# k^T v on column halves of TensorE, k's maximum by GpSimd for chunks 3 to 8, and q's transposes and k^T v issued as one piece

## The chip, the cores and the metric

The kernel runs on one core of one Trainium2 chip. The metric is device microseconds (us) of the whole launch; three runs of the kernel before gave 907.95, 908.01 and 909.28, median 908.01. No other core works beside it.

## The reference

A linear attention feeds a feed-forward layer (FFN). The inputs q, k and v have 8 batches, 8 heads, 576 rows and 64 columns; the FFN has 4608 tokens, 512 columns in and out, 2048 hidden units. All is float32.

```python
q_s = exp(q - max(q, -1)); q_s = q_s / (sum(q_s, -1) + 1e-09)
k_s = exp(k - max(k, 2)); k_s = k_s / (sum(k_s, 2) + 1e-09)
kv = einsum('bhsd,bhse->bhde', k_s, v)
x = einsum('bhsd,bhde->bhse', q_s, kv)      # then x to (4608, 512)
h = x @ w_in
g = where(h >= 1, h, where(h <= -1, 0, (h + 1) ** 2 / 4))
out = g @ w_out
```

q's maximum runs along the 64 columns of a row, k's along the 576 rows of a column.

## The kernel before

The 4608 tokens are cut into 9 chunks of 512, which the code counts from 0 (so its `c == 1` is the second chunk, and the title's chunks 3 to 8 are `c` = 2 to 7). In each chunk the FFN runs as 16 units, one for each 128 hidden units. A unit's first product (L608, tile h) is 12 matmuls of 128x512, its second (L646, tiles o) again 12; each float32 operand is split into a high and a low part in the type float32r, and three of the four products of parts are taken. Between the two products stand, on ScalarE and VectorE (ACT and DVE in the profile) in turn, `g_relu`, `g_square`, `g_min`, `g_hi` and `g_lo`; the second product needs gh, and in its third matmul gl. TensorE (PE) does the first product of the next unit before the second of this one.

The attention for chunk c+1 is worked in between, during chunk c, in four pairs of heads (`attention`, a pair is `pr`). For each pair and for `c` from 1 to 7 one batch of k and v is reduced to a 128x128 block kv, of which the two 64x64 blocks on the diagonal are wanted, one for each head:

- `k_max` (DVE) takes the maximum of the five row blocks of k, which leaves 128 partitions to be reduced. That is done on PE and DVE: `k_mt` (L382) transposes the 128x128 tile m1 into PSUM, `k_mc` (L386) takes the maximum of each row, `k_mb` (L390) transposes it back, broadcast over the partitions. `k_sub` (L394, DVE) and `k_exp` (L399, ACT) follow.
- `kv_mm` (L405) multiplies k^T by v in five float32 matmuls, each of which the profile shows as two passes, of 130 columns: 128 of v and two columns of ones, whose sum is the divisor. Of the 128x128 result half is thrown away.
- `kv_z`, `kv_hi` and `kv_lo` divide by the sum and split the blocks into parts.
- For q: `q_max` (DVE), `q_rows("qm")` (GpSimd, POOL in the profile), `q_exp` (ACT), `q_sum` (DVE), `q_rows("qrz")` (POOL), `q_tr` (L474, four transposes on PE), `q_hi`, `q_lo`, then `x_mm` (L498), `x_hi`, `x_lo`.

Chunk `c == 0` works otherwise (k comes transposed, its maximum is a free-axis one), and the ninth chunk has no k of its own. While chunk 0 runs, the weights come in as 32 pieces that ACT, DVE and POOL (`low`, L266) turn into high and low parts.

The order on each engine is fixed when the program is built. `Plan.order` is a list scheduler: each step has an engine, a booked time, a due time, and the steps it waits for; `do` gives a step its due time as a stage of its pair (`base`, in units of STEP = 5.5). Each engine then runs its own list strictly in order, so a step that waits holds up all that stand behind it. The booked times set the order alone.

Of the kernel before, what the change touches and what calls it, by code (L numbers as in the profile page):

```python
# [3 lines left out]

# [146 lines left out]
def tile_linear_attention_then_ffn(  # L151
# [18 lines left out]
    nc = tc.nc  # L170
# [122 lines left out]
    def attention(c, pr, due, step, slack):  # L293
# [52 lines left out]
        def k_max():  # L346
            kt = t["k"]
            m2 = wk.tile([P, 2, P], F32, tag="m2", name=f"m2_{n}")
            nc.vector.tensor_tensor(m2, kt[:, 0:2, :], kt[:, 2:4, :], ALU.max)
            t["m1"] = m1 = m2[:, 0, :]  # L350
# [61 lines left out]

        def kv_z():
            if first:
                z = zs = t["zs"]
            else:
                z = sm.tile([P, 1], F32, tag="z", name=f"z_{n}")
                zs = t["kv"][:, P : P + 1]
            nc.vector.tensor_scalar(z, zs, EPS, None, ALU.add)
            t["rz"] = sm.tile([P, 1], F32, tag="rz", name=f"rz_{n}")  # L420
            nc.vector.reciprocal(t["rz"], z)

        def kv_f():
            for i in range(2):
                r = slice(i * D, (i + 1) * D)
                nc.scalar.activation(
                    kvf[r, pr, r], t["kv"][r, r], AF.Copy, scale=t["rz"][r]
                )

        def kv_hi():  # L430
            for i in range(2):
                r = slice(i * D, (i + 1) * D)
                nc.scalar.activation(  # L433
                    kvt[r, c % 2, pr, 0, r], t["kv"][r, r], AF.Copy, scale=t["rz"][r]
                )

        def kv_lo():
            for i in range(2):
                r = slice(i * D, (i + 1) * D)
                nc.vector.scalar_tensor_tensor(  # L440
                    kvt[r, c % 2, pr, 1, r],
                    t["kv"][r, r],
                    t["rz"][r],
                    f32(kvt[r, c % 2, pr, 0, r]),
                    ALU.mult,
                    ALU.subtract,
                )
# [71 lines left out]
        if has_k:  # L519
            if first:  # L520
                rk, rh = room("ld kFalse", NLOAD), room("ps h", 2)
                km = do("DVE", 0.78, 0, kt_max, lk)
                ke = do("ACT", 0.95, 1, kt_exp, km)
                kz = do("DVE", 0.32, 4, kv_z, ke)
                tr = do("PE", 0.65, 2, kt_tr, ke, *rpk.wait(), *rh.wait())
                rpk.take(tr)
                rh.take(tr)
                kc = do("ACT", 0.62, 2.5, kt_copy, tr, *rk.wait())
                rk.take(kc)
                kd = do("DVE", 0.22, 2.5, kt_tail, kc)  # L530
                rh.free(kd)
                mm = do("PE", 1.15, 3.5, kv_mm, kc, kd, lv)
            else:
                rm = room("wk m2", 1)
                km = do("DVE", 1.08, 0, k_max, lk, *rm.wait(), port=True)
                rm.take(km)
                mt = do("PE", 0.25, 1, k_mt, km, *rpk.wait())
                rpk.take(mt)
                rm.free(mt)
                mc = do("DVE", 0.28, 1.5, k_mc, mt)  # L540
                mb = do("PE", 0.25, 2, k_mb, mc)
                ks = do("DVE", 0.81, 2.5, k_sub, mb)
                ke = do("ACT", 0.74, 3, k_exp, ks)
                mm = do("PE", 1.15, 3.5, kv_mm, ke, lv)
                kz = do("DVE", 0.32, 4, kv_z, mm)
            rk.free(mm)
            rv.free(mm)
            parts = [kvread.get((c - 2, pr))]
            late = START + 8 if first else 0.0
            kh = do("ACT", 0.62, 4.2, kv_hi, kz, mm, *parts, late=late)  # L550
            kl = do("DVE", 0.57, 4.4, kv_lo, kh, late=late)
            kvdone[c, pr] = kl
            if first:
                early_users.extend((mm, tr))
            kvready = [kl]
            if first:
                kf = do("ACT", 0.62, 4, kv_f, kz, mm)
                kvready = [kf]
                rpk.free(kf, kl)
            else:  # L560
                rpk.free(kl)
        qm = do("DVE", 0.68, 0.5, q_max, lq)
        qs = do("POOL", 1.05, 1, q_rows("qm", ALU.subtract), qm, port=True)
        qe = do("ACT", 0.63, 2, q_exp, qs)
        qz = do("DVE", 1.06, 2.2, q_sum, qe)
        qn = do("POOL", 1.05, 3, q_rows("qrz", ALU.mult), qz, port=True)
        tr = do("PE", 0.5, 3.6, q_tr, qn, *rpq.wait())
        rpq.take(tr)
        rq.free(tr)
# [228 lines left out]
```

## Time and profile before

| | |
|---|---|
| median of three runs | 908.01 us |
| the profiled execution, its own time | 908.67 us |
| its span, first to last instruction | 906.9 us |
| mean granted TensorE clock | 0.997 of full |
| PE busy | 888.5 us, 98% |
| DVE, ACT, POOL busy | 445.2, 431.2, 139.4 us |

A row of the timeline gives the start, the busy time, the engine, the line, what is written from what, the shapes and how many instructions were merged; in square brackets stands how long the engine was idle before, and what ended that. Busy times of matmuls overlap: what one costs on PE is the distance of the starts, not its own busy time.

### The profile page before, as it was taken

How to read it: one execution, taken by the hardware profiler on the slowest of the kernel's cores; microseconds unless marked ns; L12 is line 12 of the kernel's file. 1: busy time of each engine (PE TensorE's matmuls, PEld its weight loads, DVE VectorE, ACT ScalarE, POOL GpSimd, SP SyncE). 2: the span in 40 equal slices, each digit the busy share in tenths (PEclk: the TensorE clock that was granted, in tenths of full speed). 3: DMA queues.
4: the chain of work that ended last, by engine and by line, in shares of the span. 5: the costliest groups of instructions: out<-in, count | busy, mean ns of one | idle time of the engine just before them, and what ended most of it. 6: DMA issues, size and time to landing. Idle time of an engine off the chain costs nothing.

```text
span 906.9 us, 10847 instructions
## 1 busy us (share of the span) xinstructions
PE 888.5 (98%) x4184; PEld 734.5 (81%) x4184; DVE 445.2 (49%) x859; ACT 431.2 (48%) x736; POOL 139.4 (15%) x112
## 2 busy tenths in 40 slices
PE   6889999999999999999999999999999999999997
PEld 5568888888888888888888888888888888888885
DVE  6999975444544444444544454445444443333222
ACT  6868754443544444444444444445444444343333
POOL 5555631011101111111101110011111111000000
PEclk9999999999999999999999999999999999999999
DMA  8656512111211011011211121111100010000001
GB/s 316 199 185 218 188 52 76 42 41 41 88 41 42 29 70 34 37 42 57 73 41 42 41 88 41 41 41 68 33 28 13 27 44 12 1 12 36 1 0 47
DMA packets 24244, 57.36 MB, mean 63 GB/s; under 512 B 2688, under 2 KB 2688, under 8 KB 24192
## 3 DMA queue, kind: packets, MB, share of 16 engines
q1 hardware_dynamic: 24192, 56.67, 18.6%
q8 instruction: 33, 0.54, 0.3%
q14 instruction: 19, 0.16, 0.1%
HBM read 47.22 MB, written 9.44 MB: 62 GB/s over the span
## 4 chain that ended last, share of the span: by engine, by line
PE 89%; DVE 5%; issue 2%; ACT 1%; POOL 1%; DMA 1%; SPq 0%; DVEq 0%; POOLq 0%
PE o L646 40%; PE h L608 40%; PE kv L405 4%; PE x L498 3%; PE tp L474 2%; DVE st L252 1%; DVE st L255 1%; DVE gl L635 1%; POOL wl L266 1%; DVE r L627 1%; DMA v<-in_v 1%; PE mb L390 0%; DVE qz L467 0%; PE mt L382 0%; ACT kvt L433 0%
## 5 line engine op out<-in xcount | busy, mean ns | idle before, releaser
L627 DVE SCALAR_TENSOR_TENSOR r<-h,r 128x512 f32<-128x512 f32 x144 | 99.5, 691 | 276.2 <-ACT r L624 276.0
L608 PE MATMUL h<-xl,wh 128*128 128x512 f32 x576 | 229.7, 399 | 4.3 <-DVE r L627 3.0
L646 PE MATMUL o<-wl,gh 128*128 128x512 f32 x576 | 231.8, 402 | 0.6 <-DVE kvt L440 0.5
L646 PE MATMUL o<-wh,gl 128*128 128x512 f32 x576 | 225.8, 392 | 1.3 <-DVE gl L635 1.2
L608 PE MATMUL h<-xh,wl 128*128 128x512 f32 x576 | 225.8, 392 | 0.0
L608 PE MATMUL h<-xh,wh 128*128 128x512 f32 x576 | 225.0, 391 | 0.0
L646 PE MATMUL o<-wh,gh 128*128 128x512 f32 x576 | 224.5, 390 | 0.0
L621 ACT ACTIVATE r<-h,half 128x512 f32<-128x512 f32 x144 | 99.2, 689 | 244.3 <-PE h L608 243.5
L631 ACT CAST gh<-r 128x512 fp32r<-128x512 f32 x144 | 89.4, 621 | 88.9 <-DVE r L627 88.9
L646 PEld LDWEIGHTS o<-wh,gl 128*128 128x128 f32 x576 | 108.1, 188 | 27.3 <-DVE gl L635 4.0
L608 PEld LDWEIGHTS h<-xl,wh 128*128 128x128 f32 x576 | 108.6, 188 | 26.2 <-ACT st L249 2.1
L635 DVE TENSOR_TENSOR gl<-r,gh 128x512 fp32r<-128x512 f32 x144 | 105.4, 732 | 49.5 <-ACT gh L631 47.0
L646 PEld LDWEIGHTS o<-wl,gh 128*128 128x128 f32 x576 | 108.2, 188 | 26.0 <-ACT kvt L433 1.2
L608 PEld LDWEIGHTS h<-xh,wl 128*128 128x128 f32 x576 | 108.4, 188 | 23.6 <-POOL wl L266 0.2
L608 PEld LDWEIGHTS h<-xh,wh 128*128 128x128 f32 x576 | 108.6, 189 | 20.8 <-issue 0.2
L646 PEld LDWEIGHTS o<-wh,gh 128*128 128x128 f32 x576 | 108.4, 188 | 20.3
L457 POOL TENSOR_TENSOR q<-q,qm 128x512 f32<-128x512 f32 x36 | 52.1, 1447 | 397.1 <-DVE qm L452 395.0
L624 ACT ACTIVATE r<-r 128x512 f32<-128x512 f32 x144 | 91.0, 632 | 4.2
L457 POOL TENSOR_TENSOR q<-q,qrz 128x512 f32<-128x512 f32 x36 | 38.6, 1073 | 192.1 <-DVE qrz L469 187.2
L266 POOL TENSOR_TENSOR wl<-st,wh 128x512 fp32r<-128x512 f32 x32 | 46.0, 1453 | 39.3 <-ACT wh L262 39.3
L405 PEld LDWEIGHTS kv<-v,k 128*128 128x128 f32 (+1 forms) x320 | 41.9, 195 | 5.0 <-ACT k L375 2.1
L405 PE MATMUL kv<-v,k 128*128 128x130 f32 (+1 forms) x320 | 43.2, 281 | 1.5 <-DMA v<-in_v 1.3
(61 smaller groups left out, 594.9 us busy)
## 6 DMA issues: line engine op xcount, KB each, us to landing
st<-in_w SPq DMA_DIRECT2D x32, 512.0 KB, 4.3
v<-in_v SPq DMA_DIRECT2D x32, 325.0 KB, 3.5
q<-in_q SPq DMA_DIRECT2D x36, 256.0 KB, 2.7
out<-osb SPq DMA_DIRECT2D x36, 256.0 KB, 2.0
k<-in_k SPq DMA_DIRECT2D x28, 320.0 KB, 3.0
kt<-in_kt SPq DMA_DIRECT2D x4, 288.0 KB, 5.1
```

Of the source, the lines that this page charges most:

```text
L266: nc.gpsimd.tensor_tensor(lo, t["lw"].bitcast(F32), f32(hi), ALU.subtract)
L405: nc.tensor.matmul(t["kv"], t["k"][r, j, :], t["v"][r, j, :], start=(j == 0), stop=(j == KJ - 1),)
L457: nc.gpsimd.tensor_tensor(t["qf"], t["qf"], rows, alu)
L474: nc.tensor.transpose(t["tp"][:, j, :], t["q"][:, j, :], ident)
L498: nc.tensor.matmul(t["x"][:, :, p0:p1], lhs, rhs[:, :, p0:p1], start=(i == 0), stop=(i == 2),)
L608: nc.tensor.matmul(t["h"], lhs[:, r], rhs, start=(cc == 0 and i == 0), stop=(cc == NPAIR - 1 and i == 2),)
L621: nc.scalar.activation(t["r"], t["h"], AF.Relu, bias=half[:, :1], scale=0.5)
L624: nc.scalar.activation(t["r"], t["r"], AF.Square)
L627: nc.vector.scalar_tensor_tensor(t["r"], t["h"], 1.0, t["r"], ALU.max, ALU.min)
L631: nc.scalar.copy(t["gh"], t["r"])
L635: nc.vector.tensor_tensor(t["gl"], t["r"], f32(t["gh"]), ALU.subtract)
L646: nc.tensor.matmul(outs[c, j], lhs[:, s], rhs, start=(f == 0 and i == 0), stop=(f == NF - 1 and i == 2),)
```

## The change

Four things are changed.

1. `kv_mm` is done by heads: of k's 128 columns the first 64 go to columns 0 to 63 of PE's array and the other 64 to columns 64 to 127 (`tile_position`), each against 65 columns of v (64 and one of ones) instead of 130. Ten matmuls, 20 passes, take the place of five and ten. v's rows in memory are laid out for that; they have as many bytes as before.
2. For `c` from 2 to 7 (24 pairs) `k_all` on POOL, a maximum over all partitions that leaves its result in each of them, takes the place of `k_mt`, `k_mc` and `k_mb`. It waits for the low part of the last weight (`made[NF - 1, 1]`). `k_sub` now reads the maximum from SBUF instead of PSUM.
3. `q_tr` and `kv_mm` are one step for `c` from 1 to 7: four transposes and then the 20 passes, with the waits of both ahead of them.
4. Due times and booked times: a pair is due every 3.6 STEP instead of 4, `kv_mm`'s booked time falls from 1.15 to 0.8 (0.75 in the joint step), `k_all` is booked with 8.6.

```diff
+        def k_all():
+            nc.gpsimd.partition_all_reduce(t["mb"], t["m1"], P, bass_isa.ReduceOp.max)
...
         def kv_mm():
-            t["kv"] = kpool.tile([P, P + 2], F32, tag=ktag, name=f"kv_{n}")
+            t["kv"] = kpool.tile([P, D + 1], F32, tag=ktag, name=f"kv_{n}")
             for j in range(KJ):
                 r = slice(0, SR if first and j == KJ - 1 else P)
-                nc.tensor.matmul(
-                    t["kv"],
-                    t["k"][r, j, :],
-                    t["v"][r, j, :],
-                    start=(j == 0),
-                    stop=(j == KJ - 1),
-                )
+                for i in range(2):
+                    d = slice(i * D, (i + 1) * D)
+                    nc.tensor.matmul(
+                        t["kv"][d, :],
+                        t["k"][r, j, d],
+                        t["v"][r, j, i * (D + 1) : (i + 1) * (D + 1)],
+                        start=(j == 0),
+                        stop=(j == KJ - 1),
+                        tile_position=(0, i * D),
+                    )
...
-                mt = do("PE", 0.25, 1, k_mt, km, *rpk.wait())
-                rpk.take(mt)
-                rm.free(mt)
-                mc = do("DVE", 0.28, 1.5, k_mc, mt)
-                mb = do("PE", 0.25, 2, k_mb, mc)
-                ks = do("DVE", 0.81, 2.5, k_sub, mb)
+                if c == 1:
+                    mt = do("PE", 0.12, 1, k_mt, km, *rpk.wait())
...
+                else:
+
+                    mb = do("POOL", 8.6, 0.1, k_all, km, made[NF - 1, 1])
+                ks = do("DVE", 0.81, 2.5, k_sub, mb, port=c > 1)
...
+            def q_tr_kv_mm():
+                q_tr()
+                kv_mm()
+
+            deps = [qn, ke, lv, *rpq.wait()] + ([] if c == 1 else rpk.wait())
+            tr = mm = do("PE", 1.25, 3.6, q_tr_kv_mm, *deps)
...
-                base = 16 * c + 4 * pr - 2
+                base = 16 * c + 3.6 * pr - (1 if c == 1 else 2)
```

The order of the instructions moves at three places that matter.

PE, the pair 1 of a chunk in the steady state, around its k^T v (tile kv) and q's transposes (tile tp). Before, k^T v stands alone:

```order
L608 MATMUL h_5_2475<-xh_3_2191,wl_0_112 128x512
L405 MATMUL kv_1_2493<-v_1_2104,k_1_2101 128x130 x5
L646 MATMUL o_0_2292<-wl_1_110,gh_4_2479 128x512
L646 MATMUL o_0_2292<-wh_1_109,gh_4_2479 128x512
L646 MATMUL o_0_2292<-wh_1_109,gl_4_2485 128x512
```

Its transposes come 16 rows later, between two matmuls of the FFN. Now the two stand together, one float32 piece where there were two:

```order
L633 MATMUL h_5_2509<-xh_3_2228,wl_0_112 128x512
L481 MATMUL tp_1_2530<-ident,q_1_2145 128x128 x4
L411 MATMUL kv_1_2535<-v_1_2151,k_1_2141 64x65 x10
L671 MATMUL o_0_2351<-wl_1_110,gh_4_2507 128x512
L671 MATMUL o_0_2351<-wh_1_109,gh_4_2507 128x512
```

POOL, just behind the last weight. Before, it had only q's two steps of each pair:

```order
L457 TENSOR_TENSOR q_1_2137<-q_1_2137,qm_1_2169 128x512
L457 TENSOR_TENSOR q_1_2137<-q_1_2137,qrz_1_2240 128x512
L457 TENSOR_TENSOR q_2_2345<-q_2_2345,qm_2_2379 128x512
L457 TENSOR_TENSOR q_2_2345<-q_2_2345,qrz_2_2450 128x512
L457 TENSOR_TENSOR q_3_2541<-q_3_2541,qm_3_2573 128x512
```

Now (L386 is `k_all`, L464 q's steps; m is the tile with k's maximum):

```order
L386 ISA
L386 ISA m_2_0_1392<-m_2_0_1392 128x128
L464 ISA
L464 TENSOR_TENSOR q_1_1390<-q_1_1390,qm_1_1438 128x512
L386 ISA
L386 ISA m_2_1_1509<-m_2_1_1509 128x128
L464 ISA
L464 TENSOR_TENSOR q_1_1390<-q_1_1390,qrz_1_1524 128x512
L386 ISA
L386 ISA m_2_2_1649<-m_2_2_1649 128x128
L464 ISA
L464 TENSOR_TENSOR q_2_1600<-q_2_1600,qm_2_1660 128x512
```

The rows `ISA` without a tile are exchanges of POOL's program library, which the build puts in: `k_all` and the elementwise steps lie in different libraries. There are 24 of them ahead of a `k_all` and 24 behind one. In the first pairs, as the rows show, the `k_all` of pair 1 with both its exchanges stands between the two steps on that pair's q (qm_1, qrz_1); from pair 2 on q's two steps follow each other.

DVE, the step from the pair 0 to the pair 1 of a chunk, the closest in the program (r, gl: `g_min` and `g_lo` of units 12 and 13; L473 to L476: `q_sum` of pair 0; L350 to L353: `k_max` of pair 1):

```order
L652 SCALAR_TENSOR_TENSOR r_12_3686<-h_12_3653,r_12_3686 128x512
L426 TENSOR_SCALAR z_3_3704<-kv_3_3675 128x1
L428 RECIPROCAL rz_3_3706<-z_3_3704 128x1
L473 TENSOR_REDUCE qz_0_3713<-q_0_3535 128x8
L474 TENSOR_SCALAR qz_0_3713<-qz_0_3713 128x8
L476 RECIPROCAL qrz_0_3716<-qz_0_3713 128x8
L660 TENSOR_TENSOR gl_12_3729<-r_12_3686,gh_12_3711 128x512
L493 TENSOR_TENSOR ql_3_3734<-tp_3_3670,qh_3_3721 128x512
L447 SCALAR_TENSOR_TENSOR kvt<-kv_3_3675,rz_3_3706,kvt 64x64 x2
L350 TENSOR_TENSOR m_5_1_3745<-k_1_3692 128x256
L352 TENSOR_TENSOR m_5_1_3745<-m_5_1_3745 128x128
L353 TENSOR_TENSOR m_5_1_3745<-m_5_1_3745,k_1_3692 128x128
```

So between `q_sum` of one pair and `k_max` of the next no `g_min` of a further unit stands here; at the other three steps of a chunk one or more does. `q_exp` of pair 1 stands on ACT behind `g_square` of unit 15 and ahead of `k_exp` and `g_hi` of unit 15.

## Rows read from the trace of the kernel before

**Rows 1.** The page: busy time of each engine, share of the span, instructions.

```profile
PE 888.5 (98%) x4184; PEld 734.5 (81%) x4184; DVE 445.2 (49%) x859; ACT 431.2 (48%) x736; POOL 139.4 (15%) x112
```

**Rows 2.** The page: the chain that ended last, by engine.

```profile
PE 89%; DVE 5%; issue 2%; ACT 1%; POOL 1%; DMA 1%; SPq 0%; DVEq 0%; POOLq 0%
```

**Rows 3.** The same chain in order of time, in the last chunk: start, length, what.

```profile
824.93 2.72 PE o L646 x12
```

**Rows 4.** Groups by line and shape, PE: busy and mean ns, idle before.

```profile
L390 PE MATMUL mb<-ident,mc 128*128 128x128 f32 x28 | 7.6, 271 | 0.0
```

**Rows 5.** Timeline of PE around one transpose of k's maximum.

```profile
331.10 0.27 PE L390 MATMUL mb<-ident,mc 128*128 128x128 f32 x1
...
335.33 0.39 PE L646 MATMUL o<-wl,gh 128*128 128x512 f32 x1
```

**Rows 6.** Timeline of PE around k^T v and q's transposes of one pair.

```profile
336.69 1.28 PE L405 MATMUL kv<-v,k 128*128 128x130 f32 x10
337.73 0.48 PE L646 MATMUL o<-wl,gh 128*128 128x512 f32 x1
338.04 0.39 PE L646 MATMUL o<-wh,gh 128*128 128x512 f32 x1
...
339.89 0.60 PE L474 MATMUL tp<-ident,q 128*128 128x128 f32 x4
340.24 0.48 PE L608 MATMUL h<-xl,wh 128*128 128x512 f32 x1
340.56 0.39 PE L608 MATMUL h<-xh,wh 128*128 128x512 f32 x1
```

**Rows 7.** Timeline of PE, chunk 0: k^T v whose last two passes use 64 rows.

```profile
13.76 1.55 PE L405 MATMUL kv<-v,k 128*128 128x130 f32 x10
15.25 1.12 PE L490 MATMUL x<-q,kvf 128*128 128x512 f32 x2
```

**Rows 8.** Timeline of POOL at the start, around its only library exchange.

```profile
0.73 0.20 POOL masks.py:197 MEMSET ident<- 128x128 f32 x1 [0.29 <-POOLq L750]
1.01 0.29 POOL masks.py:199 TENSOR_SCALAR_AFFINE_SELECT ident<-ident 128x128 f32<-128x128 f32 x1
```

**Rows 9.** The page: DMA issues, KB each, median us to landing.

```profile
kt<-in_kt SPq DMA_DIRECT2D x4, 288.0 KB, 5.1
```

**Rows 10.** Timeline of ACT at the start: its table load.

```profile
0.73 1.28 ACT L740 ACT_TABLE_LOAD   x1 [0.73 <-PEq L750]
```

**Rows 11.** Timeline of POOL, one pair in the steady state.

```profile
320.95 1.55 POOL L457 TENSOR_TENSOR q<-q,qm 128x512 f32<-128x512 f32 x1 [14.95 <-DVE qm L452]
329.42 1.04 POOL L457 TENSOR_TENSOR q<-q,qrz 128x512 f32<-128x512 f32 x1 [6.92 <-DVE qrz L469]
```

**Rows 12.** The chain in order of time: x's product of one pair.

```profile
345.96 0.71 PE x L498 x6
```

**Rows 13.** The page: `g_min`, busy and mean ns, idle before.

```profile
L627 DVE SCALAR_TENSOR_TENSOR r<-h,r 128x512 f32<-128x512 f32 x144 | 99.5, 691 | 276.2 <-ACT r L624 276.0
```

**Rows 14.** Timeline of DVE: the reduction that begins `q_sum`.

```profile
328.15 0.68 DVE L466 TENSOR_REDUCE qz<-q 128x8 f32<-128x512 f32 x1
```

**Rows 15.** Timelines of DVE and PE: one unit's gl and its first use.

```profile
345.36 0.69 DVE L635 TENSOR_TENSOR gl<-r,gh 128x512 fp32r<-128x512 f32 x1
...
349.15 0.40 PE L646 MATMUL o<-wh,gl 128*128 128x512 f32 x1
```

**Rows 16.** Timeline of ACT: `k_exp` and `q_exp`.

```profile
333.73 0.74 ACT L399 ACTIVATE k<-k 128x640 f32<-128x640 f32 x1
...
350.04 0.62 ACT L462 ACTIVATE q<-q 128x512 f32<-128x512 f32 x1
```

**Rows 17.** Timeline of PE behind its longest wait in chunk 0, and that stretch by windows.

```profile
33.24 0.47 PE L608 MATMUL h<-xl,wh 128*128 128x512 f32 x1 [1.80 <-DVE r L627]
...
35.00:38.00 3.00, 2.75 (x7) 1.65 (x5) 2.99 (x5) 2.89 (x8) 2.68 (x2) 0.53 0.70 253
```

**Rows 18.** Groups by line and shape, weight loads of k^T v.

```profile
L405 PEld LDWEIGHTS kv<-v,k 128*128 128x128 f32 x312 | 40.5, 194 | 4.4 <-ACT k L375 2.1
```

More of the change, by code (lines that the diff above doesn't have):

```diff
@@ L6 @@
 import concourse.tile as tile
+from concourse import bass_isa
 from concourse import mybir
@@ L349, in k_max @@
             nc.vector.tensor_tensor(m2, kt[:, 0:2, :], kt[:, 2:4, :], ALU.max)
-            t["m1"] = m1 = m2[:, 0, :]
+            t["m1"], t["mb"] = m1, _ = m2[:, 0, :], m2[:, 1, :]
             nc.vector.tensor_tensor(m1, m1, m2[:, 1, :], ALU.max)
@@ L417, in kv_z @@
                 z = sm.tile([P, 1], F32, tag="z", name=f"z_{n}")
-                zs = t["kv"][:, P : P + 1]
+                zs = t["kv"][:, D : D + 1]
             nc.vector.tensor_scalar(z, zs, EPS, None, ALU.add)
@@ L426, in kv_f @@
                 nc.scalar.activation(
-                    kvf[r, pr, r], t["kv"][r, r], AF.Copy, scale=t["rz"][r]
+                    kvf[r, pr, r], t["kv"][r, :D], AF.Copy, scale=t["rz"][r]
                 )
@@ L433, in kv_hi @@
                 nc.scalar.activation(
-                    kvt[r, c % 2, pr, 0, r], t["kv"][r, r], AF.Copy, scale=t["rz"][r]
+                    kvt[r, c % 2, pr, 0, r], t["kv"][r, :D], AF.Copy, scale=t["rz"][r]
                 )
@@ L441, in kv_lo @@
                     kvt[r, c % 2, pr, 1, r],
-                    t["kv"][r, r],
+                    t["kv"][r, :D],
                     t["rz"][r],
@@ L531, in attention @@
                 rh.free(kd)
-                mm = do("PE", 1.15, 3.5, kv_mm, kc, kd, lv)
+                mm = do("PE", 0.8, 3.5, kv_mm, kc, kd, lv)
+                rk.free(mm)
             else:
@@ L536, in attention @@
                 rm.take(km)
-                mt = do("PE", 0.25, 1, k_mt, km, *rpk.wait())
-                rpk.take(mt)
-                rm.free(mt)
-                mc = do("DVE", 0.28, 1.5, k_mc, mt)
-                mb = do("PE", 0.25, 2, k_mb, mc)
-                ks = do("DVE", 0.81, 2.5, k_sub, mb)
-                ke = do("ACT", 0.74, 3, k_exp, ks)
-                mm = do("PE", 1.15, 3.5, kv_mm, ke, lv)
-                kz = do("DVE", 0.32, 4, kv_z, mm)
+                if c == 1:
+                    mt = do("PE", 0.12, 1, k_mt, km, *rpk.wait())
+                    rpk.take(mt)
+                    rm.free(mt)
+                    mc = do("DVE", 0.28, 1.5, k_mc, mt)
+                    mb = do("PE", 0.12, 2, k_mb, mc)
+                else:
+                    mb = do("POOL", 8.6, 0.1, k_all, km, made[NF - 1, 1])
+                ks = do("DVE", 0.81, 2.5, k_sub, mb, port=c > 1)
+                if c > 1:
+                    rm.free(ks)
+                ke = do("ACT", 0.74, 3, k_exp, ks)
+            parts = [kvread.get((c - 2, pr))]
+        qm = do("DVE", 0.68, 0.5, q_max, lq)
+        qs = do("POOL", 1.05, 1, q_rows("qm", ALU.subtract), qm, port=True)
+        qe = do("ACT", 0.63, 2, q_exp, qs)
+        qz = do("DVE", 1.06, 2.2, q_sum, qe)
+        qn = do("POOL", 1.05, 3, q_rows("qrz", ALU.mult), qz, port=True)
+        if first or not has_k:
+            tr = do("PE", 0.5, 3.6, q_tr, qn, *rpq.wait())
+        else:
+            def q_tr_kv_mm():
[3 more added lines that the diff above has]
+            tr = mm = do("PE", 1.25, 3.6, q_tr_kv_mm, *deps)
+            if c > 1:
+                rpk.take(mm)
+            kz = do("DVE", 0.32, 4, kv_z, mm)
             rk.free(mm)
+        rpq.take(tr)
+        rq.free(tr)
+        if has_k:
             rv.free(mm)
-            parts = [kvread.get((c - 2, pr))]
             late = START + 8 if first else 0.0
@@ L561, in attention @@
                 rpk.free(kl)
[L562 to L569, printed above, removed]
         if first:
@@ L769 @@
     vv = rows(inputs["v"], pad=True)
-    vv = vv.transpose(0, 1, 3, 4, 2, 5).reshape(b, NPAIR, P, KJ, 2 * D)
-    ones = np.ones((b, NPAIR, P, KJ, 2), vv.dtype)
+    vv = vv.transpose(0, 1, 3, 4, 2, 5)
+    ones = np.ones((b, NPAIR, P, KJ, 2, 1), vv.dtype)
     ones[:, :, SR:, KJ - 1] = 0
-    vv = np.concatenate([vv, ones], axis=4)
+    vv = np.concatenate([vv, ones], axis=5)
     vv = vv.reshape(b, NPAIR, P, KJ * (2 * D + 2))
```

## The prediction

> **What bounds the kernel now.** I read the page first: PE is busy for 98% of the span, DVE, ACT and POOL for 49, 48 and 15% [rows 1]. The chain that ended last is PE for 89% of the span [rows 2]. So a matmul that goes away shortens the time by what it takes of PE's issue, and work on other engines counts only where PE comes to wait for it. In the last chunk, where no attention is mixed in, twelve matmuls of the FFN take 2.72 us, 0.227 each [rows 3]; that is the pace against which an inserted piece is measured. Busy times are no measure here: a transpose of k's maximum shows 271 ns [rows 4], and adds little more than half of that (below).
>
> **The change on PE.** *k's maximum.* Where a transpose is put in, the row 18 FFN matmuls on starts at 335.33, counted from 331.10 [rows 5]: 4.23 us where 18 x 0.227 = 4.08 are due. So one costs 0.15. There are 28 `mb` [rows 4] and as many `mt`; 24 of each go: 48 x 0.15 = **7.2 us**. The low bound is a bare hand-over, 0.08 (next part): 3.8.
>
> *k^T v and q's transposes now.* k^T v costs 338.04 - 336.69 - 0.227 = 1.12, of which the ten passes to the next matmul's start are 1.04 (0.104 each) and 0.08 the hand-over back to the FFN [rows 6]. The transposes cost 340.56 - 339.89 - 0.227 = 0.44, of which four are 0.35 and the hand-over 0.09 [rows 6]. Together 1.56 for each of the 28 pairs.
>
> *k^T v and q's transposes after.* The trace has no pass on half of the columns, so its price is bounded. A pass now streams 65 columns where it streamed 130, and loads 64 weight columns where it loaded 128, so half of 0.104 is near: 0.052. If the two halves run side by side, ten such times are 0.52; if one after the other, twenty are 1.04; if halving brings nothing and nothing overlaps, 20 x 0.104 = 2.08. I take 0.52, as the halves share no column of the array and no partition of the result. PE must also change its tiling and change back. The nearest row is k^T v of chunk 0, whose last two passes use 64 rows only: 15.25 - 13.76 = 1.49 to the next piece [rows 7], against 1.04 + 0.09 for ten passes and an ordinary hand-over, so 0.36 for the change and the change back. Bounds: nothing, and twice that. The joint piece then costs 0.35 + 0.52 + 0.36 + 0.09 = 1.32 and saves 0.24; 28 x 0.24 = **6.7 us**. In chunk 0 the four k^T v pay the change of tiling already and might gain 4 x 0.5 = 2; transfers and long chains set the pace there, so I count nothing and keep the 2 for the low end.
>
> **The change on POOL.** The one new wait that matters is for POOL. A `k_all` brings two library exchanges, each of price R, and its own time A. Neither is in the trace. The only exchange before, which may find its library there already, lies between the end of the memset at 0.93 and the affine select at 1.01 [rows 8], under 0.1. That is the low bound of R. The code of another library must come from memory, and the slowest median landing of a transfer is 5.1 [rows 9]; two in a row, 10.2, are the high bound. ACT's load of its tables takes 1.28 [rows 10]. I take one landing and one such load, 6.4. For A the rows on 128 columns or more are 0.29 (affine select) [rows 8] and 1.04 to 1.55 (two operands, 512 columns) [rows 11]; I take 1.04, as it crosses partitions but has a quarter of the columns. Thus 2R + A = 13.8, between 0.5 and 22.
>
> What room is there? On average a lot: q's two steps lie 6.9 us apart now, with POOL idle, and the idle time before the first is 15 us [rows 11]. The tightest step is that from pair 0 to pair 1 of a chunk. From `q_sum` of pair 0 behind unit 12's `g_min` to `q_exp` of pair 1 behind unit 15's `g_square` PE does three units and one x product, 3 x 24 x 0.227 + 0.7 = 17.0 [rows 3, 12]. `g_min` takes 0.7 of it [rows 13], `kv_z` between the two some 0.3, `q_sum` with the hop to POOL 1.27 (328.15 to 329.42) [rows 11, 14], POOL's elementwise steps 1.04 + 1.55 [rows 11], one more hop 0.1. That leaves 12.0 for 2R + A. A later `q_exp` holds up `g_hi` and `g_lo` on ACT's and DVE's lists; gl ends at 346.05 and is first read at 349.15 [rows 15], 3.1 us later, but `q_exp` and `k_exp`, 0.62 and 0.74 [rows 16], now stand ahead of `g_hi`, so about 1.7 of it is free. PE therefore begins to wait at 2R + A = 13.7: it just fits. At the other three steps of a chunk a further unit, 5.4 us, lies between. So I charge the steady state nothing. In the first pairs both exchanges stand between q's two steps of pair 1, 13.8 us where it was 6.9 [rows 11]; the nearest row is PE's longest wait for DVE in chunk 0, 1.80 [rows 17]. I charge **1.8** once (bounds: nothing, 6.9).
>
> The Trainium skill, "GPSIMD Engine Reference", section 2.1, puts the first call to a freshly loaded kernel at approximately 6 us of code loading; as an estimate by that page 2R + A would be 13.0 and the sum the same. No row here shows it.
>
> Off the path: DVE loses 24 `k_mc`, gains nothing; `k_sub` reads two operands from SBUF, which can cost it a wait behind POOL's steps, on an engine that is 49% busy. The transfers have the same bytes. If the cover of POOL goes, ACT's list is late next, as above.
>
> **The sum.** 908.7 (the profiled execution) - 7.2 - 6.7 + 1.8 = 896.6. The profiled execution lies 0.66 above the median, so against the median 895.9: **896 us**, faster by 1.3%.
>
> **The rivals.**
>
> *POOL comes too late (slower).* For it: the 6.4 is put together from other things, the exchange may be held up by the loads of k, q and v that start at the same time, and the tightest step has no room left. Against it: only one step in four is that tight. Each microsecond of 2R + A above 13.7 costs one per chunk, six chunks. And a wait of 1.80 was followed by a stretch at a lower clock, 0.53 of full, nearly the 1.2 GHz level, with 7 matmuls in 3.0 us [rows 17], 0.2 more than 0.227 for each: 1.4 us. With R of 7.5 to 8.5 the waits come to 14 to 26 us, with the clock up to 34: 910 to 930. It turns the sign (above 909.8) at waits of 14 us in all, 2.3 per chunk, 2R + A = 16.0, or from 14.6 if each wait draws the low clock. If all steps come too late, which the 5.4 us more of the others put at about 19, 24 pairs pay, and it goes beyond 930.
>
> *The halves run one after the other.* Twenty passes at 0.052: the piece costs 1.84, 0.28 more than before. 896 + 28 x 0.52 = 910.5. For it: in the trace no two matmuls share the array. Against: they have no column in common.
>
> *The loads do not overlap either (slower).* At present the passes come 0.104 apart though a weight load alone shows 194 ns [rows 18], so loads run under the streaming of the pass before. If halves lose that, a half pass is a load and a stream, 0.052 + 0.052: 2.08 in all, and 896 + 28 x 1.56 = 940. The Trainium skill, "TensorE: Matmul & The Clock Gate", Part 3, says that LDWEIGHTS overlaps with matmuls in flight only when the row group differs; both halves use all rows, so this is the rule that speaks against the change. The whole-array passes of k^T v overlap now though all use the same rows [rows 6, 18]; no run here shows halves.
>
> *Changing the tiling costs twice the row's price.* Then k^T v loses what it gains: 896 + 28 x 0.36 = 906. If it costs nothing: 886.
>
> **How the numbers follow.** Forecast 0.50; POOL late 0.22; halves in sequence 0.13; no overlap 0.07; dear tiling 0.08. About 0.2% is what a measurement of this kernel can tell from no change, that is 906.2 to 909.8. The forecast lies on the fast side, and so do 0.05 of the dear tiling, 0.04 of POOL late and 0.01 of the halves in sequence (0.60); 0.02, 0.02 and 0.04 of these three fall within (0.08); the rest lies beyond (0.32). The range goes from 886 (tiling for nothing) to 922; outside lie the case without overlap, the late half of POOL late and the tails, 0.19. The forecast's own range is 886 to 902.
>
> **What would show it.** Right: the joint piece takes some 1.3 us from its first transpose to the FFN's pace, with two half passes starting nearly together; no `mt` or `mb` for c from 2 on; POOL shows 6 to 7 us between `k_all` and q's next step; PE waits under 1 us per chunk. Wrong: half passes 0.05 or 0.1 apart, 20 in a row; PE waits at units 15 for ACT or DVE with POOL behind them; `q_exp` waiting for POOL for several us; clock below full beyond the start.

## The result, and the profile after

899.89 us (median of four runs, 898.01 to 900.98) against 908.44 in the runs of the kernel before on the same chip (907.95 to 909.28): 0.9903 of it, 95% interval 0.9884 to 0.9922. The profiled execution is the slowest of the four, 900.98, with a span of 899.2, against 908.67 before: 7.7 less.

The page, to be laid beside [rows 1, 2]: PE is as full as before, over a shorter span, and makes up 90% of the chain. In the 40 slices of the granted clock the second one, from 22 to 45 us, is new: a 7.

```profile
PE 876.8 (98%) x4456; PEld 718.6 (80%) x4456; DVE 440.3 (49%) x835; ACT 422.7 (47%) x736; POOL 146.6 (16%) x136
...
PEclk9799999999999999999999999999999999999999
...
PE 90%; DVE 6%; ACT 2%; issue 2%; DMA 1%; SPq 0%; DVEq 0%; ACTq 0%
```

**Where time was won.** The first eviction of each chunk's output (tile osb, on ACT) marks a chunk's end. First before (start, busy, line), of the third and the fourth chunk:

```profile
329.94 0.59 ACT L700 COPY osb<-o 128x512 f32<-128x512 f32 x1 [2.83 <-PE o L646]
...
427.64 0.59 ACT L700 COPY osb<-o 128x512 f32<-128x512 f32 x1 [2.83 <-PE o L646]
```

And after:

```profile
330.91 0.59 ACT L725 COPY osb<-o 128x512 f32<-128x512 f32 x1
...
426.54 0.59 ACT L725 COPY osb<-o 128x512 f32<-128x512 f32 x1
```

97.70 us became 95.63. From the first chunk's eviction to the last chunk's, 765.9 (133.85 to 899.73) became 754.2 (137.76 to 891.95): 11.7 won. The joint step on PE, which answers to [rows 6]:

```profile
335.25 0.40 PE L633 MATMUL h<-xh,wl 128*128 128x512 f32 x1
335.48 0.60 PE L481 MATMUL tp<-ident,q 128*128 128x128 f32 x4
336.01 0.80 PE L411 MATMUL kv<-v,k 128*64 128x65 f32 x20
336.74 0.50 PE L671 MATMUL o<-wl,gh 128*128 128x512 f32 x1
337.08 0.39 PE L671 MATMUL o<-wh,gh 128*128 128x512 f32 x1
```

337.08 - 335.48 - 0.227 = 1.37 for one piece, where two cost 1.56. PE's weight loads (PEld) show what is new in it: the first half pass's load starts 0.17 late, with no other engine to wait for; behind the transposes of 26 of the 28 pairs such a gap of 0.17 stands, 4.3 us in all.

```profile
336.01 0.66 PEld L411 LDWEIGHTS kv<-v,k 128*64 128x64 f32 x20 [0.17 <-issue]
```

POOL in the steady state, in place of [rows 11]:

```profile
454.47 1.04 POOL L464 TENSOR_TENSOR q<-q,qrz 128x512 f32<-128x512 f32 x1 [8.90 <-DVE qrz L476]
462.38 0.72 POOL L386 PARTITION_ALL_REDUCE m<-m  x1 [6.87 <-DVE qm L459]
470.15 1.04 POOL L464 TENSOR_TENSOR q<-q,qm 128x512 f32<-128x512 f32 x1 [7.04 <-issue]
```

Behind the 24 `k_all` 6.7 to 7.6 us pass until q's next step, median 7.1. Ahead of them, in the 15 pairs where k's column maximum had been ready before, 5.7 to 6.9, the very first 7.4, median 6.1. With the 0.72 of `k_all` a pair's two exchanges take about 6.1 + 0.7 + 7.1 = 13.8, by the unrounded medians.

PE's rows mark no wait between 140 and 800 us. But busy times of matmuls overlap, so a late start of less than about 0.2 is not marked; the starts show one, in the first pair with a `k_all`:

```profile
141.96 0.63 ACT L469 ACTIVATE q<-q 128x512 f32<-128x512 f32 x1 [2.16 <-POOL q L464]
```

```profile
143.45 0.39 PE L633 MATMUL h<-xh,wl 128*128 128x512 f32 x1
143.78 0.50 PE L671 MATMUL o<-wl,gh 128*128 128x512 f32 x1
...
144.84 0.40 PE L671 MATMUL o<-wl,gh 128*128 128x512 f32 x1
```

`q_exp` waited for POOL, gh and then gl came late behind it, and four distances take 144.84 - 143.45 = 1.39 where 0.91 are due: 0.5 lost. Behind that, up to 800 us, PE starts nothing late.

**Where time was lost.** In the first chunk, whose eviction comes 3.9 us later (133.85 to 137.76). PE's longest waits there (start, busy, and in brackets the idle time before) answer to [rows 17]:

```profile
34.45 0.37 PE L383 MATMUL mt<-ident,m 128*128 128x128 f32 x1 [2.25 <-DVE m L353]
35.48 0.77 PE L633 MATMUL h<-xl,wh 128*128 128x512 f32 x1 [0.66 <-DVE r L652]
...
40.20 0.76 PE L671 MATMUL o<-wl,gh 128*128 128x512 f32 x1 [3.10 <-DVE kvt L447]
40.76 0.63 PE L671 MATMUL o<-wh,gh 128*128 128x512 f32 x1
41.19 0.63 PE L671 MATMUL o<-wh,gl 128*128 128x512 f32 x1
```

The matmuls behind start 0.43 apart instead of 0.23, which is the pace of the lower clock (0.52 granted from 41 to 45 us). Over the window from 28 to 48 us (busy of PE, PEld, DVE, ACT, POOL, then the granted clock, DMA share and GB/s) the granted clock was 0.91 before and is 0.74:

```profile
28.00:48.00 20.00, 13.48 (x44) 10.02 (x45) 18.61 (x32) 12.99 (x26) 10.80 (x8) 0.74 0.55 182
```

### The profile page after: what moved, and what is told of

It is laid out like the page before. It is cut to its first block, busy times and chain, and to the rows that moved or that the text cites. A ratio compares the mean times of both kernels' runs of the same rounds, so it can differ in the third digit from the quotient of the medians.

```text
span 899.2 us, 11528 instructions
## 1 busy us (share of the span) xinstructions
PE 876.8 (98%) x4456; PEld 718.6 (80%) x4456; DVE 440.3 (49%) x835; ACT 422.7 (47%) x736; POOL 146.6 (16%) x136
## 4 chain that ended last, share of the span: by engine, by line
PE 90%; DVE 6%; ACT 2%; issue 2%; DMA 1%; SPq 0%; DVEq 0%; ACTq 0%
PE o L671 42%; PE h L633 41%; PE x L505 3%; PE kv L411 2%; PE tp L481 2%; DVE st L253 1%; DVE gl L660 1%; DVE st L256 1%; DMA q<-in_q 1%; DVE r L652 0%; DVE m L350 0%; PE x L497 0%; ACT wh L263 0%; DVE qz L473 0%; ACT st L250 0%
## 5 line engine op out<-in xcount | busy, mean ns | idle before, releaser
L671 PE MATMUL o<-wl,gh 128*128 128x512 f32 x576 | 229.2, 398 | 3.2 <-DVE kvt L447 3.1
L633 PE MATMUL h<-xl,wh 128*128 128x512 f32 x576 | 226.6, 393 | 1.6 <-DVE xl L520 0.8
L464 POOL TENSOR_TENSOR q<-q,qm 128x512 f32<-128x512 f32 x36 | 38.5, 1068 | 223.0 <-issue 85.1
L464 POOL TENSOR_TENSOR q<-q,qrz 128x512 f32<-128x512 f32 x36 | 44.1, 1224 | 160.6 <-DVE qrz L476 118.4
L267 POOL TENSOR_TENSOR wl<-st,wh 128x512 fp32r<-128x512 f32 x32 | 44.2, 1394 | 48.0 <-ACT wh L263 48.0
L386 POOL PARTITION_ALL_REDUCE m<-m x24 | 17.4, 724 | 176.1 <-DVE m L353 107.8
L411 PEld LDWEIGHTS kv<-v,k 128*64 128x64 f32 (+1 forms) x640 | 23.1, 145 | 9.3 <-issue 6.0
```

The source lines that it names most:

```text
L267: nc.gpsimd.tensor_tensor(lo, t["lw"].bitcast(F32), f32(hi), ALU.subtract)
L411: nc.tensor.matmul(t["kv"][d, :], t["k"][r, j, d], t["v"][r, j, i * (D + 1) : (i + 1) * (D + 1)], start=(j == 0), stop=(j == KJ - 1), tile ...
L633: nc.tensor.matmul(t["h"], lhs[:, r], rhs, start=(cc == 0 and i == 0), stop=(cc == NPAIR - 1 and i == 2),)
L671: nc.tensor.matmul(outs[c, j], lhs[:, s], rhs, start=(f == 0 and i == 0), stop=(f == NF - 1 and i == 2),)
```

## The experiments

Three prices recur. The period is the time from the third chunk's first eviction to the fourth's (four pairs; e_all4 alone starts matmuls late in it). The piece is what k^T v and q's transposes take from PE by the distance of starts, the same in all 24 pairs but for one of e_all4. Where k^T v comes first, its first pass starts 0.32 behind the FFN's matmul instead of 0.23, and this 0.09 is counted in. The first eviction shows chunk 0. Period, piece and first eviction are from one profiled execution each. Ratios are to the kernel before, with 95% intervals.

| run | median us | ratio | period | piece | first eviction |
|---|---|---|---|---|---|
| before | 908.2 to 908.5 | 1 | 97.70 | 1.12 + 0.44 | 133.85 |
| the change | 899.89 | 0.9884 to 0.9922 | 95.63 | 1.37 | 137.76 |
| e_booked | 896.60 | 0.9862 to 0.9888 | 95.62 | 1.37 | 133.49 |
| e_old_booked | 912.44 | 1.0033 to 1.0061 | 97.71 | 1.12 + 0.44 | 136.74 |
| e_pe_max | 905.85 | 0.9963 to 0.9983 | 96.73 | 1.37 | 136.67 |
| e_whole | 904.10 | 0.9941 to 0.9966 | 96.32 | 1.56 | 135.84 |
| e_split | 896.73 | 0.9862 to 0.9889 | 95.53 | 1.32 (18), 0.93 + 0.44 (6) | 135.05 |
| e_seq | 913.31 | 1.0036 to 1.0062 | 97.30 | 1.77 | 139.83 |
| e_narrow | 905.14 | 0.9959 to 0.9985 | 96.41 | 1.56 | 137.01 |
| e_tile2 | 904.55 | 0.9953 to 0.9973 | 96.80 | 1.67 | 134.87 |
| e_all4 | 906.53 | 0.9971 to 0.9992 | 96.10 | 1.37 | 134.59 |
| e_kv_first | 895.39 | 0.9841 to 0.9868 | 95.47 | 1.32 | 133.78 |
| e_split_booked | 895.71 | 0.9850 to 0.9879 | 95.52 | as e_split | 133.13 |
| e_kv_first_c2 | 895.33 | 0.9848 to 0.9881 | 95.46 | 1.32 | 133.08 |

**The lost 3.9 us: one booked number.** In the changed kernel:

```diff
-                mm = do("PE", 0.8, 3.5, kv_mm, kc, kd, lv)
+                mm = do("PE", 1.15, 3.5, kv_mm, kc, kd, lv)
```

> One number of the changed kernel is put back: the booked time of chunk 0's k^T v, 0.8 to 1.15. It is booked for the list scheduler alone, no instruction changes. Theory A: the first eviction of chunk 0 came 3.9 us later with the change (133.85 to 137.76), because the smaller booked time turns the order of DVE's and PE's early lists, and PE waits 2.25 us for k's maximum and 3.10 us for kv_lo of chunk 0 behind it. Then that eviction comes at 134 again, the two waits are gone or under 1 us each, and the time is 899.9 - 3.9 = 896.0 (895 to 897). Rival B: it is the half passes themselves in chunk 0, each k^T v of which shows 0.9 to 1.6 us and two changes of tiling. Then the order makes no difference: 899 to 901, the first eviction still behind 137. Rival C: the low clock of that stretch comes by itself: the waits go, the time does not.

And the other way round, 1.15 to 0.8 in the kernel before:

> The kernel before with one number changed: the booked time of chunk 0's k^T v, 1.15 to 0.8, as the change has it. Theory A, this number alone turns the early lists and costs 4 us, whatever k^T v is: the first eviction comes at 137 to 138 instead of 133.85, PE waits over 2 us for k's maximum and 3 for kv_lo, and the time is 908.2 + 4 = 912 (911 to 913). Rival B, it needed the other parts of the change as well (the smaller booked times of the transposes, the joint step of chunk 1): 908 within 0.6.

Theory A, twice. Put back, the number gives 3.3 us (896.60), and the first eviction comes at 133.49. In the old kernel it costs 4.0 (912.44 against 908.48), with not one half pass in it. Its first eviction, 136.74, stays a little short of A's 137, and PE's waits of chunk 0 are those of the change:

```profile
33.12 0.33 PE L382 MATMUL mt<-ident,m 128*128 128x128 f32 x1 [2.19 <-DVE m L352]
34.15 0.47 PE L608 MATMUL h<-xl,wh 128*128 128x512 f32 x1 [0.70 <-DVE r L627]
38.87 0.76 PE L646 MATMUL o<-wl,gh 128*128 128x512 f32 x1 [3.79 <-DVE kvt L440]
```

How a number that no instruction uses does that is seen on DVE. In the change `k_max` of the first pair comes late and runs beside POOL's two `low`, 30.84 to 33.92; its three steps take 3.2 us:

```profile
31.23 1.54 DVE L350 TENSOR_TENSOR m<-k 128x256 f32<-128x256 f32 x1
32.80 1.27 DVE L352 TENSOR_TENSOR m<-m 128x128 f32<-128x128 f32 x1
34.10 0.29 DVE L353 TENSOR_TENSOR m<-m,k 128x128 f32<-128x128 f32 x1
```

With 1.15 it stands ahead of one `join`, in a gap of POOL, and takes 1.1:

```profile
27.22 0.41 DVE L350 TENSOR_TENSOR m<-k 128x256 f32<-128x256 f32 x1
27.66 0.29 DVE L352 TENSOR_TENSOR m<-m 128x128 f32<-128x128 f32 x1
27.99 0.29 DVE L353 TENSOR_TENSOR m<-m,k 128x128 f32<-128x128 f32 x1
```

PE's `mt` then waits for nothing, and PE keeps its clock: 0.91 in 28 to 48 us, as before the change. That POOL's steps are what stretches DVE's was not tried by itself.

**k's maximum back on PE and DVE.**

```diff
-                if c == 1:
+                if c >= 1:
                     mt = do("PE", 0.12, 1, k_mt, km, *rpk.wait())
```

> The changed kernel with k's maximum on PE and DVE again for all of c from 1 to 7 (two transposes and a row maximum for each pair), the rest as it is. Theory A, each transpose is worth 0.15 and POOL's exchanges keep nobody waiting: 48 x 0.15 = 7.2 more, 907.1 (906 to 908), chunks from c = 2 on 1.2 longer each. Rival B, the 24 k_all and 48 exchanges cost waits that eat part of it, at the first pairs above all (1.0 and 0.2 of wait for gl at 121 and 126): 904 to 906. Rival C, a transpose adds only the bare hand-over of 0.08: 48 x 0.08 = 3.8, 903.7.

5.96 more, just under A's range and within B's. By the period a transpose is worth (96.73 - 95.63) / 8 = 0.14 in this run. The waits that B names aren't POOL's: gl is waited for 1.0 and 0.2 us here too, at 120.3 and 125.0, with no exchange in it. But the 0.5 lost at 143.8 in the change is not here, so B is right by that much.

This run does not put the transposes back where they stood: two of a chunk's four `mt` now come right behind x's product, of which I show one, and in the kernel before none does.

```profile
347.40 0.29 PE L505 MATMUL x<-qh,kvt 128*128 128x256 f32 x1
347.52 0.27 PE L383 MATMUL mt<-ident,m 128*128 128x128 f32 x1
```

So the 0.14 holds for this order. In the kernel before, with the joint piece's gain of 1.56 - 1.37 = 0.19 taken off, the eight transposes of a chunk come to (97.70 - 95.63 - 4 x 0.19) / 8 = 0.16 each.

**k^T v on the whole array**, with everything else of the change:

```diff
-                for i in range(2):
...
-                        t["k"][r, j, d],
-                        t["v"][r, j, i * (D + 1) : (i + 1) * (D + 1)],
...
-                        tile_position=(0, i * D),
+                    t["k"][r, j, :],
+                    t["v"][r, j, :],
```

> The changed kernel with k^T v on the whole array again (five matmuls of 130 columns, ten passes), in the same place of the same joint step, with the same booked times. Theory A, the halves run side by side and gain a little: the joint piece takes 0.35 + 1.04 + 0.09 = 1.48 from its first transpose to the FFN's pace instead of 1.37, 28 x 0.11 = 3.1 more, 903.0 (902 to 904). Rival B, the halves cost the 3.9 us of chunk 0: then the first eviction of chunk 0 comes at 134 and the time is 899.9 + 3.1 - 3.9 = 899 or less. Rival C, changing the tiling eats what the halves gain: 899.9 within 0.5.

A in sign and place, 4.2 more, 0.1 above its range. The piece is 1.56, not 1.48: in one step the transposes and the five whole matmuls cost what they cost apart. By the period the halves are worth 0.69 / 4 = 0.17 a pair, so some 4.8 in 28. The first eviction varies from 135.05 to 137.76 between the runs that keep the 0.8, so one profile each can't tell what the halves themselves do to chunk 0.

**Two steps instead of one.**

```diff
-            tr = mm = do("PE", 1.25, 3.6, q_tr_kv_mm, *deps)
+            tr = do("PE", 0.5, 3.6, q_tr, qn, *rpq.wait())
+            mm = do("PE", 0.75, 3.5, kv_mm, ke, lv, *([] if c == 1 else rpk.wait()))
```

> The changed kernel with q's transposes and k^T v as two steps again, each with its own waits and due time, the k^T v by halves and k_all as they are. Theory A: apart, each piece pays its own hand-over to the FFN of 0.09, 28 x 0.09 = 2.5 more: 902.4 (901.5 to 903.5). Rival B: the joint step pays for its single hand-over with waits, since it needs q and k at once: no wait of PE at it shows in the steady state, so this would have to show in the first pairs; apart is then as fast or faster, 898.5 to 900. Rival C: apart, each half-array piece pays more than a hand-over, because the transposes no longer stand next to it: more than 904.

A fell, and B was too timid: 3.2 less. In 18 of 24 pairs the scheduler puts the two side by side anyway, k^T v first, and then they cost 1.32 instead of 1.37. In the six others they cost 0.93 + 0.44, no more than the joint piece. So joining saves nothing on PE. Of the 4.5 us between the two profiled executions 2.7 lie in chunk 0 and 1.3 in chunk 1. That is the same early stall in other clothes, as the run with both edits shows:

> Both repairs at once: two steps for q's transposes and k^T v, and the booked time of chunk 0's k^T v at 1.15. Alone they gave 896.7 and 896.6, against 899.9. Theory A, they mend different places (the early lists; the first pairs behind them, where the joint step's chunk 1 took 96.7 against 95.4 apart): the first eviction at 133.5, the last one 754.2 - 1.3 - 0.6 = 752.4 behind it, so 885.9 instead of 887.2: 895.3 (894.5 to 896). Rival B, both mend the same stall in chunk 0: 896.6 within 0.5. Rival C, apart is worth more in chunk 0 once the lists are right: below 894.5.

(The edit is that of e_split and that of e_booked together.) 895.71: only 0.9 is left of the 3.2 once the booked number is right. The time lies in A's range, but not for A's reason: the 1.3 of chunk 1 is 0.1 here (96.03 against e_booked's 96.13). The 0.9 is 0.4 in chunk 0 and 0.1 in each of six chunks, the piece's order. So for the stall B holds.

**The order within the joint step**, on top of the booked number:

```diff
-                q_tr()
                 kv_mm()
+                q_tr()
```

> The kernel with the booked time put back to 1.15 (896.6), and in the joint step k^T v ahead of q's transposes instead of behind them. In the run with two steps the pieces stood in that order in 18 pairs and cost 1.33 of PE's time, against 1.38 for transposes first. Theory A, the order of the two alone is worth it: 28 x 0.05 = 1.4 less, 895.2 (894.5 to 896). Rival B, apart with own waits is what was worth it: 896.6 and the piece still at 1.38.

A: 895.39, the piece 1.32 in all 24 pairs. Why this order is cheaper was not followed. Then the same with the step split for c = 1 alone:

```diff
-            tr = mm = do("PE", 1.25, 3.6, q_tr_kv_mm, *deps)
+            if c == 1:
+                tr = do("PE", 0.5, 3.6, q_tr, qn, *rpq.wait())
+                mm = do("PE", 0.75, 3.5, kv_mm, ke, lv)
+            else:
...
+                tr = mm = do("PE", 1.25, 3.6, q_tr_kv_mm, *deps)
```

> The run with k^T v ahead of the transposes (895.4), with the joint step only from c = 2 on; for c = 1, whose pairs are worked in chunk 0, the two steps apart. Theory A, the joint step costs time only in chunk 0, where q's and k's chains are late in turn and one of them holds up the other: 0.5 to 2 less, 893.4 to 894.9. Rival B, it costs nothing there once the booked time is right: 895.4 within 0.5.

B: 895.33, no difference. With 895.4 these two are the fastest of both kernels and all variants.

**What makes a half pass cheap.** Two runs on top of the booked number (896.60). First, the five matmuls of the first head ahead of those of the second:

```diff
-            for j in range(KJ):
-                r = slice(0, SR if first and j == KJ - 1 else P)
-                for i in range(2):
+            for i in range(2):
...
+                for j in range(KJ):
```

> The kernel with the booked time at 1.15 (896.6), and k^T v with all five matmuls of the first head ahead of the five of the second, instead of in turn. Theory A, the halves run side by side because they come in turn on different columns: now only one half of the array works at a time, so twenty half passes of 0.062 take 1.24 instead of 0.62: 28 x 0.62 = 17 more, 914 (910 to 916). Rival B, a half pass is short of itself, whatever stands next to it: 896.6 within 0.6, the piece still at 1.38. Rival C, each change from one half to the other costs: then this is faster, below 896.

A: 913.31. In the same place as above:

```profile
340.31 0.60 PE L481 MATMUL tp<-ident,q 128*128 128x128 f32 x4
340.84 1.20 PE L411 MATMUL kv<-v,k 128*64 128x65 f32 x20
341.97 0.50 PE L671 MATMUL o<-wl,gh 128*128 128x512 f32 x1
342.31 0.40 PE L671 MATMUL o<-wh,gh 128*128 128x512 f32 x1
```

The piece is 342.31 - 340.31 - 0.227 = 1.77, 0.40 more than in turn. So the halves do run side by side. Pass by pass in the traces, the half passes of one head start 0.058 apart in both runs; in turn, those of the other head start with them. The gain is 0.4, not 0.62, because here too the second head's first passes start beside the first head's last: the last of the twenty starts 0.98 behind the first, where 19 x 0.058 = 1.10 would be due (in turn it is 0.57). 24 x 0.40 is 9.6; 6.3 more are lost in chunk 0 (first eviction 139.83), which was not followed further.

Second, the whole array against half of v's columns:

```diff
-                        t["k"][r, j, d],
-                        t["v"][r, j, i * (D + 1) : (i + 1) * (D + 1)],
+                    t["k"][r, j, :],
+                    t["v"][r, j, : D + 1],
```

> The kernel with the booked time at 1.15 (896.6), and k^T v on the whole array again, but against the 65 columns of v of the pair's first head alone: the product of the second head is left out. So 128 weight columns are loaded as in the kernel before, half as many columns are streamed, and PE changes no tiling. Theory A, a pass goes by the columns it streams: ten passes of 0.052, the joint piece 0.44 + 0.52 + 0.09 = 1.05 instead of 1.38, 28 x 0.33 = 9 less, 887.5 (886 to 889). Rival B, a pass goes by the weights it loads: ten passes of 0.104 as in the whole-array run, the piece at 1.57, 28 x 0.19 = 5.3 more, 902 (901 to 903), and the half pass is cheap because it loads 64 weight columns.

B. The weight loads and the passes of this piece:

```profile
336.10 1.20 PEld L409 LDWEIGHTS kv<-v,k 128*128 128x128 f32 x10
```

```profile
335.77 0.60 PE L478 MATMUL tp<-ident,q 128*128 128x128 f32 x4
336.21 1.23 PE L409 MATMUL kv<-v,k 128*128 128x65 f32 x10
337.24 0.48 PE L668 MATMUL o<-wl,gh 128*128 128x512 f32 x1
```

Ten passes take 337.24 - 336.21 = 1.03 with 65 columns streamed, as they did with 130 (1.04, [rows 6]): half the streaming saves nothing. What a pass costs here goes by its weights: passes of 128 weight columns start 0.11 apart pass by pass, those of 64 0.058, at 65 streamed columns both. (The half passes also use another tiling of the array; no run has 64 weight columns without it.) The Trainium skill, "TensorE: Matmul & The Clock Gate", section on LDWEIGHTS, gives a load as the weight columns over 1.2, in ns, whatever the rows: as an estimate 107 and 53 ns, within a tenth of both. (The median is 3 us above B's 902, by chunk 0: the first eviction, 137.01, comes 3.5 later than e_booked's with the same booked number. Why was not followed.)

**What a change of tiling costs.** q's transposes in the middle of k^T v:

```diff
                 for i in range(2):
...
+                if not first and j == 2:
+                    q_tr()
...
             def q_tr_kv_mm():
-                q_tr()
                 kv_mm()
```

> The kernel with the booked time at 1.15, and q's four transposes in the middle of k^T v, behind its third pair of matmuls: PE now changes its tiling twice as often, nothing else is added. Compared with the run that has k^T v ahead of the transposes (895.4, piece at 1.33). Theory A, a change and the change back cost 0.32, as worked out from 1.38 = 0.35 + 0.62 + 0.32 + 0.09: one more pair of changes, 28 x 0.32 = 9 more, 904.4 (903 to 906). Rival B, a change costs nothing of its own and the 0.32 is a start-up of the passes or of their weight loads: under 28 x 0.1 = 3 more, 895.4 to 898.

A: 9.2 more than e_kv_first, the piece 0.35 longer (1.67 against 1.32), 28 x 0.35 = 9.8.

```profile
334.18 0.39 PE L634 MATMUL h<-xh,wl 128*128 128x512 f32 x1
334.50 0.57 PE L411 MATMUL kv<-v,k 128*64 128x65 f32 x12
335.00 0.66 PE L483 MATMUL tp<-ident,q 128*128 128x128 f32 x4
335.59 0.45 PE L411 MATMUL kv<-v,k 128*64 128x65 f32 x8
335.97 0.50 PE L672 MATMUL o<-wl,gh 128*128 128x512 f32 x1
```

The next FFN matmul starts at 336.31, so with the 0.09 ahead the piece is 336.31 - 334.18 - 2 x 0.227 = 1.67. From the transposes to the half passes it takes 0.59, where the next FFN matmul follows after 0.35 [rows 6]. The Trainium skill, "TensorEngine Tiling (Array Packing)", Key Properties, says that changing the tiling mode drains TensorE. The trace agrees in so far as the load of the first half pass behind the transposes starts 0.17 late. This run doesn't tell a drain from a start-up that every group of half passes would pay: k^T v has two groups here. Whole passes behind the transposes pay neither (e_whole: piece 1.56, as apart).

**POOL's room.**

```diff
-            nc.gpsimd.partition_all_reduce(t["mb"], t["m1"], P, bass_isa.ReduceOp.max)
+            for _ in range(4):
+                nc.gpsimd.partition_all_reduce(t["mb"], t["m1"], P, bass_isa.ReduceOp.max)
```

> The kernel with the booked time at 1.15 (896.6), and k_all issued four times in a row for each of the 24 pairs: 3 x 0.72 = 2.2 more of POOL's time between the two exchanges and no more exchanges. Measured before: 6.0 ahead, 0.72, 7.1 behind, 13.8 together, and no wait of PE in the steady state. Theory A, that is at the limit which the prediction worked out (13.7): PE then waits for gl once per chunk, some 2.2 each in six chunks, 13 in all, with a low clock behind some of them: 909 to 916. Rival B, POOL has room left on that step: under 3 us more, 896.6 to 899.5. Rival C, all four steps of a chunk are as tight: 24 x 2.2 = 53 more.

Neither: 9.9 more. Of that, 7.4 fall in chunk 1 (its period 103.5 instead of 96.1), where the first pairs come close together; the largest loss is that PE waits 4.29 us for gh behind a `q_exp` that waited 7.70 for POOL:

```profile
176.45 0.80 PE L672 MATMUL o<-wl,gh 128*128 128x512 f32 x1 [4.29 <-ACT gh L657]
```

```profile
174.64 0.63 ACT L470 ACTIVATE q<-q 128x512 f32<-128x512 f32 x1 [7.70 <-POOL q L465]
175.17 0.72 ACT L404 ACTIVATE k<-k 128x640 f32<-128x640 f32 x1
175.80 0.60 ACT L657 CAST gh<-r 128x512 fp32r<-128x512 f32 x1
```

In the steady state a chunk pays 0.6 on average (96.10, 96.70 and 96.72 against 95.62, 95.87 and 96.27), at the step from pair 0 to pair 1 alone. There the two exchanges and four `k_all` took 16.2 (314.80 to 331.03):

```profile
313.49 1.31 POOL L465 TENSOR_TENSOR q<-q,qrz 128x512 f32<-128x512 f32 x1 [4.59 <-ACT qh L490]
320.88 3.12 POOL L387 PARTITION_ALL_REDUCE m<-m  x4 [6.07 <-DVE gl L661]
331.03 1.03 POOL L465 TENSOR_TENSOR q<-q,qm 128x512 f32<-128x512 f32 x1 [7.04 <-issue]
```

```profile
332.10 0.63 ACT L470 ACTIVATE q<-q 128x512 f32<-128x512 f32 x1 [2.25 <-POOL q L465]
```

```profile
333.51 0.39 PE L634 MATMUL h<-xh,wl 128*128 128x512 f32 x1
333.92 0.50 PE L672 MATMUL o<-wl,gh 128*128 128x512 f32 x1
```

and the first matmul on gh, at 333.92, started 0.41 behind the one ahead of it instead of 0.23: 0.2 late. So the wait begins at about 16.0 in the steady state, and the change stands some 2 us inside it there. In its first pair it stands just outside (the 0.5 above).

## Why the prediction was right, and where it was not

Forecast 896 (886 to 922), faster; measured 899.89. The mechanism was right, one term was left at nothing that cost 3.9, and one was charged at 1.8 that cost 0.5. That the 3.9 left the time in the range is luck: the range was wide for POOL's sake, and held no price for chunk 0.

- *PE bounds it, work taken off PE counts.* Right: PE is busy 98% again, and in the steady state none of its starts is late.
- *k's maximum, 0.15 a transpose, 7.2.* Nearly right: 0.14 by the period of the run that undoes it, in another order of the transposes, and 5.96 by the medians; 0.16 worked out for the order of the kernel before.
- *The joint piece, 1.32, 6.7.* Nearly: 1.37. A pair of half passes side by side takes 0.058, not 0.052, ten of them 0.58; with 0.35 for the transposes 0.44 is left for the change of tiling and the hand-over, where 0.45 was taken. So it saves 0.19 where 0.24 was forecast, 28 x 0.05 = 1.4 less. The period from the kernel before to e_pe_max, (97.70 - 96.73) / 4 = 0.24, is no confirmation, since that run also has its transposes in cheaper places. The whole steady state agrees all the same, 2.07 a chunk where 4 x 0.24 + 8 x 0.15 = 2.16 were forecast: what the piece lacks the transposes bring. Two reasons fell. I halved the pass because both its streamed and its weight columns are halved; the weight columns alone count. And I counted one hand-over saved by joining; nothing is saved.
- *POOL, 2R + A = 13.8, "it just fits".* The sum measured 13.8 (R 6.1 ahead and 7.1 behind, A 0.72), where 2 x 6.4 + 1.04 was put together from other things: that it comes out the same is in part luck, the single terms being 0.3 to 0.7 off. The limit of 13.7 was wrong, it is about 16.0: between `q_sum` and `q_exp` I counted three units and an x product, and left out the joint piece itself, 1.4, which PE does there as well. The slack behind is larger too, 2.25 - 0.2 = 2.1 instead of 1.7; the other 0.5 is open. The approximately 6 us of the Trainium skill, "GPSIMD Engine Reference", section 2.1, agree with the exchange ahead of `k_all` and lie 1 us under the one behind; a time of this size is paid at each of the 48 exchanges.
- *First pairs, 1.8.* Too much: 0.5 is lost, in pair 0, where `q_exp` waits for POOL, and not between q's two steps of pair 1. The larger waits just ahead, 1.0 and 0.2 for gl, come without `k_all` too.
- *Chunk 0: "transfers and long chains set the pace there, so I count nothing".* This is the step that failed. I read the lists on PE, POOL and DVE at the places the change is about, and took the booked times as setting "the order alone", hence free. In chunk 0 DVE is nearly full (95% busy from 50 to 120 us), and PE's next step often stands right behind one of DVE's: there the order is the time. One booked number cost 3.3 to 4.0 us, a third of what the rest won. It is not all that moves chunk 0: e_narrow and e_seq are 3.5 and 6.3 late there with the number put right.
- *The sum.* 765.9 - 754.2 = 11.7 won behind the first chunk, where 12.96 for its 24 pairs less 1.8 for the first pairs, 11.2, were forecast; the difference is chunk 0, 3.9 lost where 1 was to be won. Even with the number put right the first eviction gains only 0.4 (133.85 to 133.49).

The rivals: halves one after the other is what e_seq is, 1.77 where 1.84 was priced. The rule of the Trainium skill, "TensorE: Matmul & The Clock Gate", Part 3, that loads overlap only when the row group differs, does not hold in that form here: both halves use the same rows, and two loads and two passes go by in the 0.058 that one of them takes. Dear tiling fell: 0.44 with the hand-over, not 0.81. POOL too late is the nearest: 2.4 us more on each `k_all` take back 9.9 of the 11.6 that e_booked wins.

## What to carry to other kernels

A number that only feeds a scheduler is an edit like any other: compare the order where an engine is nearly full and the one that bounds stands behind it, above all in the start-up. Before halving a small matmul ask whether its pass is paid by streamed columns or by weight columns. Putting two small pieces side by side saved nothing here (1.37 against 0.93 + 0.44), but their order was worth 0.05 a pair. And where busy times overlap, a short wait shows only in the distance of the starts: here 0.1 late cost 0.5.

## What was not expected of the hardware

- Float32 passes of k^T v start 0.11 us apart with 128 weight columns, whether 65 or 130 columns are streamed, and 0.058 with 64; two halves of the array in turn run at that pace each.
- A further change of tiling and back cost 0.35 us, and on the way in the weight load started 0.17 late.
- GpSimd's exchange took 5.7 to 6.9 us towards `k_all` (the first 7.4) and 6.7 to 7.6 back; `k_all` itself, a maximum over 128 partitions of 128 columns, only 0.72.
- Two DVE steps of 0.41 and 0.29 took 1.54 and 1.27 beside GpSimd's subtractions; that these are the cause was not tried.
